# Key-value products of a linear-attention block: diagonal blocks of 32 by 32 instead of 64 by 64

## The chip, the cores and the metric

The kernel runs on one core of a Trainium2 chip. The metric is the device time of one execution in microseconds; the time before is the median of three runs, 482.34 us (482.19 to 482.75).

## The reference

One transformer block in float32 on a sequence of 2048 rows of 512 values, conditioned by a vector c (six modulation vectors sa, ca, ga, sb, cb, gb come from it).

```python
h = _layernorm(x) * (1 + ca) + sa
x = x + ga * A(h)                     # linear attention, 32 heads of 16 values
h = _layernorm(x) * (1 + cb) + sb
x = x + gb * B(h)                     # dense 512 -> 1792, mish, dense 1792 -> 512
# A:  q, k, v = h @ wqkv, by heads
phi = lambda t: where(t > 0, t + 1, exp(t)) + 1e-6
kv  = einsum("bhsd,bhse->bhde", phi(k), v)      # a 16 x 16 matrix for each head
z   = einsum("bhsd->bhd", phi(k))
num = einsum("bhqd,bhde->bhqe", phi(q), kv)
den = einsum("bhqd,bhd->bhq", phi(q), z) + 1e-6
A   = (num / den) @ wo
```

## The kernel before

The whole work is written out by hand: Python emits one instruction after the other, and each engine runs its own in that order, so the order in the program is the order of the work. Generators (`spawn`, `spawn_idle`, `tick`) put the work of the other engines between the matmuls of TensorE (PE): each `tick()` moves every running generator one `yield` on. DMAs are issued from SP's queue (hardware) and from GpSimd's (POOL, software). Large products are made of three float32r products of upper and lower halves (`mm3`, `split`: the upper half is a copy, mostly on ScalarE, ACT; the lower half a subtraction on VectorE, DVE). A few small products are done in plain float32; in the trace each of those calls leaves two weight-load records and two matmul records.

The sequence is worked on in blocks b of 512 rows and tiles t of 128. Up to some 103 us the kernel computes phi(k) and accumulates `gacc`, the 512 by 512 product of the normalized x and phi(k) over all rows. From it come `zs[k]` (four tiles of 128 by 512, `kv_side`, L1128), which stand for h transposed times phi(k). Then q is computed for blocks 0 and 1 (`q_sevens`, L1146; its last results are the `cq` of L408).

The place of the change is L1149 to L1166, at 125 to 132 us. In order of the program:
- `attend(0, 3)` begins (L1149): the denominators `den`, 16 float32 products with 32 weight columns and 128 moving columns, in four column blocks of the array (L926).
- `kv_ps` (L1151 to L1156): for each of four groups g of 128 columns (8 heads) and each k, the product of `wv[k]` and `zs[k]` for diagonal blocks only, 64 by 64 (j = 0, 1); 32 calls. The bank `kv_ps` is one of four of the tag `acc`.
- `run(early_rows[0])` (L1157): ACT and DVE finish splits of MLP weights (`a_0l`, `s_0l`).
- the masks (L1158 to L1162): VectorE multiplies the diagonal blocks by `bmask` (1 inside a head's 16 by 16 block, 0 outside) into `kv`, which was set to zero at the start (L154).
- `split` of kv: `kvh` on ScalarE, `kvl` on VectorE (L1163, L1166). Between the two, `attending` goes one step on: `rden` and its reciprocal on VectorE (L930, L931), `rden_d` to DRAM and `rd`, its broadcast, back (L933, L937), issued from GpSimd for blocks 0 and 1.

After it come q for block 2 (`q_unit`, three PSUM banks `h`), the products `m_ps` of kv and wo (L1179), `attend(1, 4)`, q for block 3, and then the output products `o_unit` (L974 to L983) whose weights are `qs`, the halves of phi(q) divided by its denominator (L945, L946, L88). The normalized rows of the first blocks are turned through VectorE's transposes (`wide_n`) and DMAs (`sq_n`); the small steps of that are `rs_n` (VectorE and GpSimd, L1001, L199), `nb_n` (L1004) and `n` (ACT, L208). `gb_row`, `gb_d`, `gb_bc` (L454 to L458) broadcast one modulation row over GpSimd's queue. At 192 us the MLP's first products `p_a` begin (`pairs_begin`, L1247), with `b_0l`, a lower half that VectorE makes (L88), and from there the MLP takes the rest.

Of the kernel before, what the change touches and what calls it, by code (L numbers as in the profile page):

```python
# [11 lines left out]
ALU = mybir.AluOpType  # L12

P = 128
# [11 lines left out]
def block_kernel(ctx: ExitStack, tc: tile.TileContext, x, wqkv, wo, w1, b1t, w2, c, wmodt, out):  # L26
    nc = tc.nc
    act, dve, pool, pe, sp = nc.scalar, nc.vector, nc.gpsimd, nc.tensor, nc.sync
# [13 lines left out]
    def ps(tag, name, shape=(P, 512)):  # L42
        return psp.tile(list(shape), F32, tag=tag, name=name, bufs=PBUFS[tag])
# [24 lines left out]
    def run(gen):  # L68
        for _ in gen:
            pass  # L70
# [7 lines left out]
    def split(name, t, keep, key, lo_engine=dve, hi_engine=act, plus=None):  # L78

        hi, lo = sb(f"{name}h", F32R, t.shape), sb(f"{name}l", F32R, t.shape)  # L80
        if hi_engine is act:
            act.activation(hi, t, AF.Copy)
        else:
            hi_engine.tensor_copy(hi, t)
        if lo_engine is dve:
            yield
        if plus is None:
            lo_engine.tensor_tensor(lo, t, f32(hi), op=ALU.subtract)  # L88
        else:
            dve.scalar_tensor_tensor(lo, t, plus, f32(hi), op0=ALU.add, op1=ALU.subtract)  # L90
        keep[key] = hi, lo
# [55 lines left out]
    bmask = cst.tile([P, P], F32, name="bmask")  # L147
# [540 lines left out]
    wv, wos = {}, {}  # L688
# [17 lines left out]
    zs = {}  # L706
# [444 lines left out]
    kv_ps = ps("acc", "kv_ps")  # L1151
    for g in range(4):
        for k in range(4):
            for j in range(2):
                cs = slice(P * g + 64 * j, P * g + 64 * (j + 1))
                pe.matmul(kv_ps[64 * j:64 * (j + 1), cs], wv[k][:, cs], zs[k][:, cs], start=k == 0, stop=k == 3)  # L1156
    run(early_rows[0])  # L1157
    for j in range(2):  # L1158
        js = slice(64 * j, 64 * (j + 1))
        dve.tensor_tensor(kv.rearrange("p (g m) -> p g m", g=4)[js, :, js],  # L1160
                          kv_ps.rearrange("p (g m) -> p g m", g=4)[js, :, js],
                          bmask[js, js].unsqueeze(1).to_broadcast([64, 4, 64]), op=ALU.mult)  # L1162
    kv_halves = split("kv", kv, kvs, 0)  # L1163
    next(kv_halves)
    next(attending)
# [500 lines left out]
```

## Time and profile before

| | |
|---|---|
| median of three runs | 482.34 us |
| the profiled execution | 482.34 us |
| its span, first to last instruction | 480.6 us |
| TensorE busy (matmuls) | 473.1 us, 98%, 2290 records |
| weight loads (PEld) | 387.9 us, 81%, 2290 records |
| VectorE busy | 392.1 us, 82% |
| ScalarE busy | 309.9 us, 64% |
| GpSimd busy | 135.9 us, 28% |

All views are of one profiled execution. PE is the matmul side of TensorE, PEld its weight loads, which run beside the matmuls; matmuls are pipelined, so records of one engine overlap. A timeline merges neighbouring records of one line and shape and gives their number (x64) and the time from the first start to the last end. "Idle before" is the time in which an engine stood still, with the instruction whose end released it; "issue" means that nothing in the profile explains it.

### The profile page before, as it was taken

The page shows a single profiled execution, that of the slowest core. Times are in us where ns is not written, and L with a number is a line of the kernel's source. Part 1 is how long each engine was busy: PE and PEld are TensorE (multiplying, and loading weights), DVE is VectorE, ACT ScalarE, POOL GpSimd, SP SyncE. Part 2 cuts the span into 40 slices and gives each one's busy share as a digit, 9 for nine tenths or more (in the row PEclk, how much of TensorE's full clock was granted, in tenths as well). Part 3 has the DMA queues.
Part 4 walks back from the last instruction along what each step waited for, and adds up shares of the span by engine and source line. Part 5 has one row for each costly group of instructions (what it writes and reads, how often), then busy time and mean ns, then how long its engine had stood idle before and what let it go on. Part 6 is the DMA issues. An engine that isn't in the chain of part 4 may idle for free.

```text
span 480.6 us, 7101 instructions
## 1 busy us (share of the span) xinstructions
PE 473.1 (98%) x2290; PEld 387.9 (81%) x2290; DVE 392.1 (82%) x786; ACT 309.9 (64%) x556; POOL 135.9 (28%) x233
## 2 busy tenths in 40 slices
PE   7999999999999999999999999999999999999997
PEld 6778786868887888888888888888888888888887
DVE  6989897998899899698879874798544787779992
ACT  6977558756667977587787756694156677637700
POOL 3586242000022255112224425343011101354400
PEclk9999999999999999999999999999999999999999
DMA  8904649443766356927538759999643503487974
GB/s 304 383 15 83 115 111 241 131 153 91 240 184 178 84 125 182 324 86 242 175 111 233 249 156 307 369 310 280 188 119 87 118 15 88 110 218 155 242 156 106
DMA packets 81280, 84.92 MB, mean 177 GB/s; under 512 B 23473, under 2 KB 55737, under 8 KB 81242
## 3 DMA queue, kind: packets, MB, share of 16 engines
q1 hardware_dynamic: 55176, 47.08, 34.0%
q0 software_dynamic: 23808, 36.59, 28.4%
q10 hardware_dynamic: 2258, 0.79, 0.8%
q8 instruction: 18, 0.29, 0.2%
q14 instruction: 20, 0.16, 0.1%
HBM read 55.32 MB, written 22.81 MB: 163 GB/s over the span
## 4 chain that ended last, share of the span: by engine, by line
PE 83%; DVE 5%; DMA 4%; POOL 2%; ACT 2%; issue 2%; SPq 1%; DVEq 0%; POOLq 0%; ACTq 0%
PE p_a L1234 15%; PE o L981 9%; PE p_s L1234 8%; PE oacc L74 5%; PE oacc L76 5%; PE oacc L75 5%; PE m L76 5%; PE m L74 5%; PE m L75 5%; PE p L1234 4%; PE pq_a L397 2%; DMA ku<-ku 2%; PE pq L74 2%; PE pq L76 2%; PE pq L75 2%
## 5 line engine op out<-in xcount | busy, mean ns | idle before, releaser
L1239 DVE TENSOR_TENSOR cb<-p_s,u 128x512 f32<-128x512 f32 x28 | 19.2, 687 | 12.2 <-ACT u L1287 10.6
L820 POOL DMA_DIRECT2D wb<-w2d x14 | 9.8, 704 | 65.2 <-PE m L76 28.3
L1226 ACT ACTIVATE ub<-cb,b1c 128x512 f32<-128x512 f32 x28 | 20.1, 720 | 9.0 <-DVE cb L1239 8.7
L1562 POOL DMA_DIRECT2D wt_m<-w2t x20 | 14.0, 702 | 25.1 <-PE m L76 16.8
L199 POOL TENSOR_TENSOR rs_n<-rs_n,half 128x1 f32<-128x1 f32 x16 | 9.7, 609 | 36.0 <-DVE rs_n L225 19.1
L1244 ACT ACTIVATE p<-p_a 128x512 f32<-128x512 f32 x12 | 7.0, 582 | 19.7 <-PE p_a L1234 11.7
L933 POOL DMA_DIRECT2D rden_d<-rden x2 | 1.5, 733 | 61.6 <-DVE rden L931 61.6
L1287 ACT ACTIVATE u<-p_a 128x512 f32<-128x512 f32 x14 | 8.4, 597 | 13.8 <-PE p_a L1234 13.6
L1201 ACT ACTIVATE u<-p,b1c 128x512 f32<-128x512 f32 x14 | 9.6, 684 | 11.7 <-PE p L1234 11.7
L1201 ACT ACTIVATE u<-p_a,b1c 128x512 f32<-128x512 f32 x14 | 9.6, 687 | 8.5 <-PE p_a L1234 8.3
L826 POOL DMA_DIRECT2D w2b<-w2d x20 | 10.6, 540 | 13.9 <-PE oacc L76 8.2
L270 ACT ACTIVATE hf_n<-sq_n,mc 128x512 f32<-128x512 f32 x16 | 12.0, 804 | 0.7 <-DMA w2r<-in_w_dram 0.7
L304 DVE SCALAR_TENSOR_TENSOR ku<-e_k,relu_k 128x512 f32<-128x512 f32 x16 | 10.9, 684 | 1.2 <-ACT relu_k L302 1.2
L304 DVE SCALAR_TENSOR_TENSOR q<-e_q,relu_q 128x512 f32<-128x512 f32 x16 | 10.7, 687 | 1.4 <-ACT relu_q L302 1.4
L199 POOL TENSOR_TENSOR rs_x<-rs_x,half 128x1 f32<-128x1 f32 (+1 forms) x10 | 7.8, 785 | 13.2 <-DVE rs_x L194 12.3
L190 DVE BATCH_NORM_STATS2 st_x<-x 128x6 f32<-128x512 f32 x13 | 8.8, 676 | 3.1 <-DMA x<-in_x_dram 3.1
L256 POOL DMA_DIRECT2D sq_n<-wide_n x16 | 8.7, 553 | 6.8 <-DVE wide_n L239 4.7
L175 DVE SCALAR_TENSOR_TENSOR wm<-wm,sc_row 128x512 f32<-128x512 f32 x16 | 10.5, 684 | 0.0
L945 DVE SCALAR_TENSOR_TENSOR q<-q,rd 128x512 f32<-128x512 f32 x16 | 10.4, 683 | 0.1
L256 POOL DMA_DIRECT2D sq_x<-wide_x x16 | 8.9, 566 | 5.0 <-DVE wide_x L239 4.6
L301 ACT ACTIVATE e_k<-pk 128x512 f32<-128x512 f32 x16 | 9.4, 590 | 1.3 <-PE pk L76 1.3
L759 DVE TENSOR_TENSOR w2g<-w2r,gb_bc 128x256 f32<-128x256 f32 x28 | 10.0, 416 | 0.0
(1622 smaller groups left out, 1884.8 us busy)
## 6 DMA issues: line engine op xcount, KB each, us to landing
wm<-in_wmodt_dram SPq DMA_DIRECT2D x24, 256.0 KB
w1p<-in_w_dram SPq DMA_DIRECT2D x24, 256.0 KB
w2b<-w2d POOLq DMA_DIRECT2D x20, 256.0 KB, 6.8
wt_m<-w2t POOLq DMA_DIRECT2D x20, 256.0 KB, 3.6
r<-in_x_dram SPq DMA_DIRECT2D x16, 256.0 KB
x<-in_x_dram SPq DMA_DIRECT2D x15, 256.0 KB
w2r<-in_w_dram SPq DMA_DIRECT2D x14, 256.0 KB
wb<-w2d POOLq DMA_DIRECT2D x14, 256.0 KB, 3.6
```

The source lines that it names most:

```text
L74: pe.matmul(o, st[0], mv[0], start=start, stop=False)
L75: pe.matmul(o, st[0], mv[1], start=False, stop=False)
L76: pe.matmul(o, st[1], mv[0], start=False, stop=stop)
L199: pool.tensor_tensor(y, y, half[:, lo:hi], op=ALU.pow)
L256: queues[n % len(queues)].dma_start(v[32 * m:32 * (m + 1), :, a, :], w[32 * a:32 * (a + 1), m:16:4].rearrange("p j t c -> p j (t c)"))
L304: dve.scalar_tensor_tensor(dst, e, 1.0, r, op0=ALU.min, op1=ALU.add)
L981: pe.matmul(p, l, r, start=not seeded and g == 0 and i == 0, stop=g == 3 and i == 2, skip_group_check=seeded)
L1201: act.activation(u, p, AF.Mish, bias=b1c[:, f:f + 1])
L1226: act.activation(u, p, AF.Mish, bias=b1c[:, f:f + 1])
L1234: pe.matmul(p, st, mv, start=onto is None and c == 0 and i == 0, stop=c == 1 and i == 2, skip_group_check=onto is not None)
L1239: dve.tensor_tensor(out, p, u, op=ALU.add)
L1562: pool.dma_start(v, w2t[g][:, :, SUM[name], :])
```

## The change

```diff
     for g in range(4):
         for k in range(4):
-            for j in range(2):
-                cs = slice(P * g + 64 * j, P * g + 64 * (j + 1))
-                pe.matmul(kv_ps[64 * j:64 * (j + 1), cs], wv[k][:, cs], zs[k][:, cs], start=k == 0, stop=k == 3)
+            for j in range(4):
+                cs = slice(P * g + 32 * j, P * g + 32 * (j + 1))
+                pe.matmul(kv_ps[32 * j:32 * (j + 1), cs], wv[k][:, cs], zs[k][:, cs], start=k == 0, stop=k == 3)
     run(early_rows[0])
-    for j in range(2):
-        js = slice(64 * j, 64 * (j + 1))
+    for j in range(4):
+        js = slice(32 * j, 32 * (j + 1))
         dve.tensor_tensor(kv.rearrange("p (g m) -> p g m", g=4)[js, :, js],
                           kv_ps.rearrange("p (g m) -> p g m", g=4)[js, :, js],
-                          bmask[js, js].unsqueeze(1).to_broadcast([64, 4, 64]), op=ALU.mult)
+                          bmask[js, js].unsqueeze(1).to_broadcast([32, 4, 32]), op=ALU.mult)
```

The products outside the heads' blocks are masked away in both versions, so fewer of them are computed: 64 calls with 32 weight columns and 32 moving columns in place of 32 calls with 64 and 64. A mask instruction covers 32 partitions and four groups of 32 columns, in place of 64 partitions and four groups of 64.

## Rows read from the trace of the kernel before

**Rows 1.** The page, busy us (share of the span) and records of TensorE.

```profile
PE 473.1 (98%) x2290; PEld 387.9 (81%) x2290; DVE 392.1 (82%) x786; ACT 309.9 (64%) x556; POOL 135.9 (28%) x233
```

**Rows 2.** Waits of weight loads, 126.4 to 478: us in total, times, longest.

```profile
PEld den L926 <- issue: 0.7, 2, 0.4
...
PEld den L926 <- DVE q L304: 0.4, 1, 0.4
...
PEld p_a L75 <- DVE b_0l L88: 0.2, 1, 0.2
PEld kv_ps L1156 <- issue: 0.2, 1, 0.2
```

**Rows 3.** By stretch: length, busy PE, PEld, DVE, ACT, POOL, clock, DMA share, GB/s.

```profile
126.40:153.70 27.30, 27.30 (x206) 22.49 (x203) 27.15 (x59) 16.64 (x35) 6.77 (x11) 1.00 0.64 186
...
192.40:477.30 284.90, 284.88 (x1296) 237.65 (x1295) 220.38 (x419) 172.04 (x303) 73.17 (x126) 1.00 0.68 187
```

**Rows 4.** TensorE, 125.3 to 128.5: timeline (start, length), then ns of one (min/median/max).

```profile
125.36 1.08 PE L926 MATMUL den<-q,hmask 128*32 128x128 f32 x32
126.37 2.08 PE L1156 MATMUL kv_ps<-zs,wv 128*64 128x64 f32 x64
...
L1156 PE MATMUL kv_ps<-zs,wv x64: 221/222/271, 126.4 to 128.2; 128*64 128x64 f32 x64
L926 PE MATMUL den<-q,hmask x128: 272/273/298, 125.4 to 172.9; 128*32 128x128 f32 x128
```

**Rows 5.** Timeline of den's weight loads up to 125.359, 125.385 and 125.410.

```profile
125.36 0.11 PEld L926 LDWEIGHTS den<-q,hmask 128*32 128x32 f32 x1 [0.35 <-issue]
...
125.36 0.13 PEld L926 LDWEIGHTS den<-q,hmask 128*32 128x32 f32 x4 [0.35 <-issue]
...
125.36 0.16 PEld L926 LDWEIGHTS den<-q,hmask 128*32 128x32 f32 x8 [0.35 <-issue]
```

**Rows 6.** Timeline of VectorE around the masks, 128.7 to 130.0.

```profile
128.76 0.42 DVE L88 TENSOR_TENSOR a_0l<-w1p,a_0h 128x256 fp32r<-128x256 f32 x1
...
129.10 0.85 DVE L1160 TENSOR_TENSOR kv<-kv_ps,bmask 64x256 f32<-64x256 f32 x2
...
129.98 0.35 DVE L930 TENSOR_SCALAR rden<-den,tiny_den 128x128 f32<-128x128 f32 x1
```

**Rows 7.** The masks alone: ns of one (min/median/max), first and last start.

```profile
L1160 DVE TENSOR_TENSOR kv<-kv_ps,bmask x2: 406/416/427, 129.1 to 129.5; 64x256 f32<-64x256 f32 x2
```

**Rows 8.** Timelines of VectorE and of TensorE's weight loads at 149.5 to 150.6.

```profile
149.48 0.69 DVE L88 TENSOR_TENSOR qs_2l<-q,qs_2h 128x512 fp32r<-128x512 f32 x1
...
150.55 0.19 PEld L981 LDWEIGHTS o<-m_2h,qs_2l 128*128 128x128 f32 x1
```

**Rows 9.** Timelines of GpSimd (143.9 to 157.7) and of VectorE at 158.3.

```profile
143.91 0.71 POOL L933 DMA_DIRECT2D rden_d<-rden  x1 [6.54 <-DVE rden L931]
...
157.10 0.59 POOL L458 DMA_DIRECT2D gb_bc<-gb_d  x1 [4.67 <-DMA gb_d<-gb_row]
157.70 0.60 POOL L199 TENSOR_TENSOR rs_n<-rs_n,half 128x1 f32<-128x1 f32 x1
...
158.33 0.16 DVE L1004 SCALAR_TENSOR_TENSOR nb_n<-osum,rs_n 128x1 f32<-128x1 f32 x1 [0.51 <-POOL rs_n L199]
```

**Rows 10.** Waits of ScalarE from 158 to 182: us, times, longest.

```profile
ACT n L208 <- DVE nb_n L1004: 3.8, 2, 2.9
```

**Rows 11.** Waits of VectorE from 126.4 to 195.

```profile
DVE wide_n L239 <- ACT n L208: 1.4, 2, 1.1
```

**Rows 12.** Timelines of VectorE and of TensorE's weight loads at 192 us.

```profile
191.67 0.69 DVE L88 TENSOR_TENSOR b_0l<-hf_n,b_0h 128x512 fp32r<-128x512 f32 x1
...
192.41 0.19 PEld L75 LDWEIGHTS p_a<-b_0l,a_0h 128*128 128x128 f32 x1 [0.21 <-DVE b_0l L88]
```

**Rows 13.** By stretch, as rows 3: the DMA share behind the masks.

```profile
136.50:147.50 11.00, 11.00 (x77) 8.75 (x76) 10.93 (x24) 5.81 (x11) 1.58 (x3) 1.00 0.99 285
```

**Rows 14.** Waits of SP's queue from 128 to 145: us, times, longest.

```profile
SPq L103 <- PE m_ps L76: 9.1, 2, 8.7
```

## The prediction

> **What bounds the kernel now.** I read the page's busy shares first: TensorE is busy 98% of the span [rows 1]. Shares say nothing of one stage, so the next view is what TensorE's weight loads waited for from 126.4 us, where the changed products begin, to the last matmul. Two entries name another engine. A den load waited 0.4 us for VectorE's q, but two other den loads show the same idle time as "issue", 0.7 us for both: that is TensorE's own change of array shape. A load for p_a waited 0.2 us for VectorE's b_0l, and this one I take as a wait [rows 2]. The table by stretch agrees: behind that wait TensorE is busy 284.88 of 284.90 us [rows 3]. So whatever moves TensorE's arrival there, or b_0l, moves the end by as much. The reader is to see two things at once: TensorE is the bound, and it meets VectorE at 192.4 us with nothing to spare. Before that, from 126.4 to 153.7, VectorE is itself busy 27.15 of 27.30 us [rows 3]: in the stage of the change there are two full engines.
>
> The profiled execution took 482.34 us around a span of 480.6, and 482.34 is also the median of the three runs, so the sum is made against it directly.
>
> **Part 1, the products.** 32 calls become 64, and as each call leaves two records (64 now), 64 records become 128. Now: the first record of kv_ps starts at 126.37 and they end 2.08 us later; one takes 0.222 us, so 31 steps of two (one for each column block) take 2.08 - 0.22 = 1.86 us, 0.060 us a step [rows 4]. The den products beside it have the array shape that the change will use, 32 columns, four blocks: 1.08 - 0.27 = 0.81 us over 7 steps of four is 0.116 us a step [rows 4]. At the granted clock of 1.00 [rows 3], the 2.4 GHz level, that is 278 cycles for 128 moving columns and 144 for 64, so about two cycles a column and some 0.007 to 0.009 us more. A step of four with 32 moving columns is then 64 cycles, 0.027 us, plus 0.008: 0.035 us. Another limit lies close: four den loads have started 0.02 us after the first, eight after 0.05 us, so some 0.007 us each [rows 5], and four of these are 0.028. Bounds for a step: 0.028 below, 0.116, den's whole step, above. I take 0.035, worked out from the two rows of the same engine and type. 31 steps: 1.09 us in place of 1.86, a gain of 0.77. Also, loads for kv_ps idle 0.20 us at the change from 32 columns to 64, where nothing but issue is named [rows 2]; with 32 columns behind 32 an ordinary step of 0.116 stands there, a gain of 0.09. The change of shape towards pq stays. **TensorE gains 0.86 us** (1.08 at the lower bound; at the upper it loses 1.65).
>
> **Part 2, the masks.** Two VectorE instructions of 64 partitions by 256 columns become four of 32 by 128. Now: 0.406 and 0.427 us [rows 7], together 0.85 us, and rden starts 0.88 after the first [rows 6]. They lie end to end. The 256-wide a_0l in front does not: it lasts 0.42 and kv starts 0.34 behind it [rows 6]. A column costs (0.68 - 0.42)/256 = 1.0 ns, by the 512-wide qs_2l [rows 8] and a_0l, so 128 columns less make 0.42 into 0.28. If end to end stays: four of 0.28 and four gaps of about 0.02 are 1.20 us, **0.32 more than 0.88**. If they overlap as a_0l and kv do: four steps of 0.34 - 0.13 = 0.21 are 0.84, 0.04 less. If rden's 0.35 for 128 columns from PSUM [rows 6] is the right length: 1.48, 0.60 more. I take +0.32: kv's own row is the nearest.
> The Trainium skill (VectorE: DVE Perf Modes, "Two Vector instructions with no wait between them") has a rule against this part: an instruction that starts on another group of 32 partitions than the one before it is held until all earlier ones have finished. By it three masks and rden are held instead of one mask and rden, and the sum would be the +0.32; without it, the -0.04.
>
> What is queued behind: on VectorE rden and all that follows, on ScalarE kvh, which reads kv, and on GpSimd the rden_d transfer. No DMA is added or moved, and the mask's constant is only sliced otherwise.
>
> **What each is worth at the end.** VectorE's queue from 126.4 to 153.7 has 0.15 us left for all its waits together [rows 3]: it gets next to nothing from TensorE's 0.86 us, and carries the 0.32 along. The first place where TensorE meets it: qs_2l runs 149.48 to 150.17 and its weight load starts at 150.55 [rows 8]. That is 0.38 us of room up to the load, and up to 0.19 more as far as the load, 0.19 long, runs ahead of the matmuls: I take the middle, 0.47, so TensorE can come 0.47 us earlier if VectorE stays, and 0.47 - 0.32 = 0.15 with the masks. The rest of the 0.86 turns into a wait for qs_2l.
> Then b_0l. I followed it back. VectorE's second rden releases GpSimd's rden_d at 143.91; behind its landing come the rd loads and gb_d, a wait of 4.67 us for gb_d's landing, gb_bc at 157.10 and rs_n at 157.70; for that VectorE idles 0.51 and goes on at 158.33 [rows 9]. From there the waits that I see are ScalarE's for VectorE's nb_n (3.8 us) [rows 10] and VectorE's for ScalarE's n (1.4 us) [rows 11]: the two release each other up to b_0l, 191.67 to 192.36, whose load starts at 192.41 [rows 12]. So +0.32 at rden is +0.32 at b_0l, if the transfer keeps its length. It may not: rden_d lands out of a full DMA system (0.99 busy from 136.5 to 147.5 [rows 13]), and part of this traffic is released on SP by TensorE's m_ps products [rows 14], which come 0.86 earlier. A transfer issued later into the same backlog lands less than 0.32 later. I keep +0.32 as the upper and 0 as the lower end, and as the issue itself moves by all of it, take 0.25.
>
> **Sum:** TensorE's 0.86 is lost at qs_2l and b_0l, and b_0l comes 0.25 later: 482.34 + 0.25 = 482.6 us.
>
> **The rivals.**
> - *TensorE's gain comes through* (faster side). It needs b_0l to come 0.86 earlier: 482.34 - 0.86 = 481.5, or 481.3 with 0.028 us a step. For it: TensorE is the bound at all other places. Against: VectorE's row without idle time [rows 3].
> - *The masks overlap.* Then VectorE is 0.04 earlier, and a DMA backlog that clears sooner may let 158.33 come up to 0.5 earlier (the idle 0.51 of [rows 9]). TensorE is still held by qs_2l, at 0.47 + 0.04 = 0.51 earlier: 482.34 - 0.04 = 482.3, or 481.8 at best.
> - *Issue becomes TensorE's bound* (slower side). kv_ps now passes one record per 0.030 us and den one per 0.029 (their steps over two and four); no row shows a lasting rate above that, only short bursts [rows 5]. If that is a limit per record, 128 records take 31 x 0.116 = 3.60 us, 1.65 more with the shape change, and as TensorE has nothing to spare at 192.4, the end is 1.65 later: 484.0. It decides from a step above 0.035 + 0.86/31 = 0.063 us on, where TensorE itself gets late. Against it: two cycles a column explains both rows by streaming alone.
> The Trainium skill (TensorE: Matmul & The Clock Gate, "Wait — 56ns, not 53.3ns?") states such a floor, about 25 ns from start to start however small a matmul is. By that rule 128 records would take 3.2 us and the end would be some 1.3 later. The 0.007 us between den's loads speaks against it as a floor over all four column blocks.
> - *A larger mask price*, 0.60, with the transfer in full: 482.9; inside my case.
>
> **How the numbers follow.** About 0.2%, 0.96 us, is what a measurement of this kernel can tell from no change. My case 0.72, overlapping masks 0.15, issue bound 0.07, TensorE's gain in full 0.06. My case runs from 482.3 (backlog hides it) to 482.9 and with the spread of the three runs of before (482.19 to 482.75) to 483.2; overlap reaches to 481.8. The range 481.8 to 483.2 leaves out the last two rivals. Slower by over 0.96 us: the issue bound and 0.02 of my case, 0.09. Faster by over 0.96 us needs the gain in full at the lower bound of a step, or the DMA timing to fall well: 0.04. The rest, 0.87, is no change.
>
> **What would show each step.** Right: 128 kv_ps records in about 1.1 us with no shape idle behind den; four masks end to end in about 1.2 us, kvh and rden 0.3 later; TensorE now waits for qs_2l (0.7 us, where it had none), and the p_a load still starts just behind b_0l, at 192.4 to 192.8. Wrong: TensorE without waits up to the end and a span of 479.7 (gain through); kv_ps over 3 us (issue); masks 0.2 apart (overlap); b_0l well ahead of its load (another wait decides).

## The result and the profile after

The changed kernel takes 484.03 us (median of 8 runs, 483.15 to 484.45), the kernel before 482.62 in the same comparison (8 runs). The ratio is 1.0029 with a 95% interval of 1.0021 to 1.0037: **slower by 1.4 us**, where 482.6 was forecast and 483.2 was the upper end (0.25 more than the 482.34 from which the forecast started). The profiled execution has a span of 482.5 us against 480.6, so the trace shows a loss of 1.9.

First the two edited parts. The timelines of TensorE and VectorE after, as [rows 4, 6]:

```profile
125.69 1.08 PE L926 MATMUL den<-q,hmask 128*32 128x128 f32 x32
126.59 1.28 PE L1156 MATMUL kv_ps<-zs,wv 128*32 128x32 f32 x128
127.80 0.50 PE L74 MATMUL pq<-hT_x_0h,wq_0h 128*128 128x512 f32 x1
...
129.10 0.42 DVE L88 TENSOR_TENSOR a_0l<-w1p,a_0h 128x256 fp32r<-128x256 f32 x1
129.43 1.18 DVE L1160 TENSOR_TENSOR kv<-kv_ps,bmask 32x128 f32<-32x128 f32 x4
130.65 0.35 DVE L930 TENSOR_SCALAR rden<-den,tiny_den 128x128 f32<-128x128 f32 x1
```

Note first that `den`, the last work ahead of the change, already starts 0.33 us later than in the profile of before (125.36): this one execution brought that along, and it has to be taken off every difference below. Then: 128 records of kv_ps in 1.28 us, and rden 1.22 us behind the first mask, where it was 0.88.

Next, what the weight loads waited for, from 120 to 480 us (in us in total, times, longest; [rows 2] has the same before, from 126.4):

```profile
PEld o L981 <- DVE qs_2l L88: 1.8, 2, 1.0
PEld den L926 <- issue: 1.1, 3, 0.4
PEld p_a L75 <- DVE b_0l L88: 0.8, 1, 0.8
```

TensorE now waits 1.8 us for qs_2l, in two waits (1.0 up to 150.9 us and 0.8 up to 192.5), and 0.8 in place of 0.2 for b_0l. Behind that it waits for nothing, as before. The chain to b_0l, in the timelines of GpSimd and VectorE and the last matmul of TensorE:

```profile
144.58 0.71 POOL L933 DMA_DIRECT2D rden_d<-rden  x1 [6.53 <-DVE rden L931]
150.91 2.36 POOL L937 DMA_DIRECT2D rd<-rden_d  x4 [5.62 <-ACT relu_q L302]
159.02 0.59 POOL L458 DMA_DIRECT2D gb_bc<-gb_d  x1 [5.22 <-DMA gb_d<-gb_row]
...
160.26 0.16 DVE L1004 SCALAR_TENSOR_TENSOR nb_n<-osum,rs_n 128x1 f32<-128x1 f32 x1 [0.66 <-POOL rs_n L199]
...
193.60 0.68 DVE L88 TENSOR_TENSOR b_0l<-hf_n,b_0h 128x512 fp32r<-128x512 f32 x1
...
478.92 0.28 PE L76 MATMUL m<-wt_m,l_m_4l 128*128 128x256 f32 x1
```

The same places before: GpSimd's first rd and the last matmul here, the rest in [rows 9, 12].

```profile
149.54 2.36 POOL L937 DMA_DIRECT2D rd<-rden_d  x4 [4.92 <-ACT gb_row L454]
...
477.00 0.28 PE L76 MATMUL m<-wt_m,l_m_4l 128*128 128x256 f32 x1
```

| step | later than before, us | added there |
|---|---|---|
| den (ahead of the change) | 0.33 | 0.33, this execution |
| rden_d issued (second rden) | 0.67 | 0.34, the masks |
| rd issued, behind rden_d's landing | 1.37 | 0.70, transfer |
| gb_bc issued, behind gb_d's landing | 1.92 | 0.55, transfer |
| nb_n, b_0l, last matmul | 1.93, 1.93, 1.92 | 0 |

So nothing more is lost behind 160 us, and TensorE lost nothing in its own work. Some 1.25 us come from two transfers that got longer, more than the masks cost.

A second path ends almost together with this one. VectorE's last product ahead of nb_n, q<-q,rd (L945), needs the rd loads; it ends at 157.82 before and at 159.59 after, 1.77 us later. Before and after, in VectorE's timeline:

```profile
153.73 1.50 DVE L945 SCALAR_TENSOR_TENSOR q<-q,rd 128x512 f32<-128x512 f32 x2
...
156.53 1.29 DVE L945 SCALAR_TENSOR_TENSOR q<-q,rd 128x512 f32<-128x512 f32 x2
```

```profile
154.66 0.69 DVE L945 SCALAR_TENSOR_TENSOR q<-q,rd 128x512 f32<-128x512 f32 x1 [0.19 <-DMA rd<-rden_d]
156.31 0.69 DVE L945 SCALAR_TENSOR_TENSOR q<-q,rd 128x512 f32<-128x512 f32 x1 [0.96 <-DMA rd<-rden_d]
...
158.31 1.28 DVE L945 SCALAR_TENSOR_TENSOR q<-q,rd 128x512 f32<-128x512 f32 x2
```

GpSimd's small rs_n ends 0.41 to 0.48 us behind the end of that q in all nine traces in which rs_n starts ahead of it and nb_n waits for rs_n, the one of before among them. So without gb_d's longer transfer nb_n would still have come some 1.7 us later (estimate: 1.77, less the 0.05 between the 0.48 of before and the 0.43 usual). Most of the loss is in rden_d (0.70) and in rd behind it (1.77 - 1.37 = 0.40); gb_d counts for some 0.2.

The view of DMA issues gives the same as time from issue to landing, for the kernel before and the changed one (stretch 142 to 160 us; KB each, median us):

```profile
rd<-rden_d POOLq DMA_DIRECT2D x4, 256.0 KB, 4.8
...
rden_d<-rden POOLq DMA_DIRECT2D x1, 64.0 KB, 5.1
gb_d<-gb_row POOLq DMA_DIRECT2D x1, 2.0 KB, 5.0
```

```profile
rd<-rden_d POOLq DMA_DIRECT2D x4, 256.0 KB, 5.2
...
rden_d<-rden POOLq DMA_DIRECT2D x1, 64.0 KB, 5.8
gb_d<-gb_row POOLq DMA_DIRECT2D x1, 2.0 KB, 5.5
```

Something else had moved the other way: SP's queue. Before and after, its loads in the full DMA stretch:

```profile
137.34 0.33 SPq L103 DMA_DIRECT2D wm<-in_wmodt_dram  x1
...
139.64 2.20 SPq L103 DMA_DIRECT2D wm<-in_wmodt_dram  x2
```

```profile
136.74 0.33 SPq L103 DMA_DIRECT2D wm<-in_wmodt_dram  x1
...
139.04 2.19 SPq L103 DMA_DIRECT2D wm<-in_wmodt_dram  x2
```

They wait for TensorE's m_ps [rows 14], so they come 0.60 us earlier, 0.93 without the 0.33. GpSimd's rden_d comes 0.67 later, behind them. That gave the theories. A: the early products release SP's loads, which stretch the chain's transfers, and the masks cost their own size (later D: what stretches the transfers is the load of SP's transfers). B: the masks' delay alone does it (later E: the late issue alone). C: it is chance.

One thing has to be added to A. The same eight SP loads (wm, r and w1p) are issued ahead of rden_d in both kernels, by 143.3 us. What differs is what they meet: before, the first of them is issued as GpSimd has just issued the rd loads of the block ahead (134.96 to 137.37 us); after, it comes 1.3 us before the end of these issues (135.64 to 138.05). The slowest of those rd loads took 9.4 us from issue to landing, 7.1 before.

### The profile page after: what moved, and what is told of

Read it like the earlier page. It is cut to its first block, busy times and chain, and to the rows that moved or that the text cites. A ratio compares the mean times of both kernels' runs of the same rounds, so it can differ in the third digit from the quotient of the medians.

```text
span 482.5 us, 7228 instructions
## 1 busy us (share of the span) xinstructions
PE 473.6 (98%) x2354; PEld 386.6 (80%) x2354; DVE 392.4 (81%) x788; ACT 310.0 (64%) x556; POOL 136.2 (28%) x233
## 4 chain that ended last, share of the span: by engine, by line
PE 72%; DVE 11%; DMA 5%; issue 4%; ACT 4%; POOL 3%; SPq 0%; DVEq 0%; POOLq 0%; ACTq 0%
PE p_a L1234 15%; PE p_s L1234 8%; PE oacc L76 5%; PE oacc L74 5%; PE oacc L75 5%; PE m L76 5%; PE m L74 5%; PE m L75 5%; PE p L1234 4%; PE pq_a L397 2%; DMA ku<-ku 2%; PE o L981 2%; PE pk L76 1%; DMA rden_d<-rden 1%; DMA gb_d<-gb_row 1%
## 5 line engine op out<-in xcount | busy, mean ns | idle before, releaser
L945 DVE SCALAR_TENSOR_TENSOR q<-q,rd 128x512 f32<-128x512 f32 x16 | 10.3, 682 | 1.1 <-DMA rd<-rden_d 1.1
```

## The experiments

Times are against the kernel before, run beside each on the same chip. The columns on the right are of one profiled execution each, whose own time stands beside the median: e12's and e7's are slow ones of their runs, e14's a quick one. "rden_d" is the second one's time from issue to landing, "b_0l to end" the distance from b_0l's start to the end of the last matmul.

| run | ratio (95%) | us, median | profiled, us | rden_d, us | b_0l starts | b_0l to end |
|---|---|---|---|---|---|---|
| before | | 482.62 | 482.34 | 5.1 | 191.67 | 285.61 |
| change | 1.0029 (1.0021 to 1.0037) | 484.03 | 484.26 | 5.8 | 193.60 | 285.60 |
| e1 masks only | 1.0017 (1.0008 to 1.0026) | 483.64 | 483.01 | 5.2 | 192.33 | 285.62 |
| e2 half the products | 1.0014 (1.0006 to 1.0023) | 483.39 | 483.32 | 5.8 | 192.63 | 285.62 |
| e7 change, two masks | 1.0016 (1.0006 to 1.0026) | 483.18 | 483.93 | 5.6 | 193.25 | 285.62 |
| e3 change, work put off | 0.9989 (0.9981 to 0.9998) | 482.11 | 482.63 | 3.3 | 191.95 | 285.62 |
| e4 before, work put off | 1.0005 (0.9996 to 1.0014) | 483.10 | 483.10 | 3.8 | 192.42 | 285.62 |
| e5 change, w1p late | 1.0126 (1.0112 to 1.0140) | 488.94 | 488.65 | 4.0 | 197.96 | 285.61 |
| e6 before, w1p late | 1.0109 (1.0095 to 1.0123) | 487.98 | 488.42 | 4.7 | 197.72 | 285.63 |
| e8 change, put off, w1p late | 1.0133 (1.0118 to 1.0149) | 489.01 | 488.34 | 3.0 | 197.63 | 285.65 |
| e9 change, w1p mid | 1.0017 (1.0008 to 1.0026) | 483.69 | 484.12 | 4.9 | 193.40 | 285.62 |
| e10 before, w1p mid | 0.9999 (0.9990 to 1.0008) | 482.45 | 482.16 | 4.0 | 191.33 | 285.77 |
| e11 change, put off, w1p mid | 1.0009 (0.9992 to 1.0026) | 482.63 | 482.60 | 3.0 | 191.89 | 285.65 |
| e12 change, on GpSimd | 0.9989 (0.9979 to 0.9998) | 482.39 | 483.16 | 6.1 | 192.45 | 285.62 |
| e13 before, on GpSimd | 0.9992 (0.9983 to 1.0000) | 482.50 | 482.50 | 4.7 | 191.70 | 285.74 |
| e14 change, r late | 1.0013 (1.0002 to 1.0024) | 483.19 | 482.36 | 3.6 | 191.63 | 285.63 |
| e15 before, r late | 0.9993 (0.9984 to 1.0002) | 482.17 | 482.09 | 3.8 | 191.37 | 285.66 |
| e16 change, r late, on GpSimd | 0.9987 (0.9977 to 0.9997) | 481.62 | 482.02 | 4.2 | 191.35 | 285.61 |
| e17 change, r late, put off | 1.0014 (1.0002 to 1.0027) | 483.25 | 482.64 | 3.2 | 191.96 | 285.63 |
| e18 before, r late, on GpSimd | 0.9992 (0.9983 to 1.0001) | 482.38 | 482.21 | 3.8 | 191.40 | 285.75 |

The last column is the first finding: where TensorE waits for b_0l, the end stands 285.60 to 285.65 us behind b_0l's start, whatever was done before it; where it does not wait (e8, e10, e13, e15, e18) the distance is 285.65 to 285.77. Where TensorE waits, b_0l sets the end.

**One half of the change at a time (e1, e2).** e1 leaves the products as before and has only the four masks. e2 has `range(2)` for k and `stop=k == 1` in the kernel before, so it leaves out half of the key-value sum; TensorE is early and VectorE is not late.

> The mask in four pieces of 32 rows, the products as before in blocks of 64. VectorE is late by the masks' 0.34 us, TensorE is not early, so SP's loads behind m_ps are issued as before. Theory A (TensorE's early products release SP's loads earlier, and these stretch the rden_d and rd transfers): the masks' delay alone costs its own size, +0.2 to +0.4 us, and rden_d and rd keep their lengths. Theory B (VectorE's late issue alone meets a worse moment of the DMA backlog): +1.2 to +1.6 us, all of the change's loss. Theory C (the longer transfers are what one run of DMA happened to do): 0 to +0.4.

> Only two of the four products of each group of key-value columns are made, in blocks of 64; two masks as before. It leaves out half of the key-value sum. TensorE is early by 16 steps of 0.060 us, 0.96 us, VectorE is not late. If the chain through rden keeps its times, TensorE waits for qs_2l and b_0l and the time is 0 to -0.3 us. Theory A: SP's loads come about 0.6 us earlier, rden_d and rd land later, +0.6 to +1.2 us. Theory B: 0 to -0.3. Theory C: 0 to -0.3.

Measured: +0.82 us by the ratio's 0.0017 for the masks, +0.68 for the early products, and 1.5 together, the change's 1.4. A had the second right and the first too small, B and C had both wrong. So each part of the change costs by itself; as each ratio is known to about 0.45 us, the shares are rough. The trace of e1: rden_d keeps its length (5.2) and is issued 0.43 us later (0.10 of it already ahead of the change), gb_bc comes 0.41 later, nb_n 0.66. The 0.24 between the last two seem to come from GpSimd's small rs_n, 0.60 us before [rows 9]:

```profile
157.51 0.59 POOL L458 DMA_DIRECT2D gb_bc<-gb_d  x1 [4.51 <-DMA gb_d<-gb_row]
158.12 0.84 POOL L199 TENSOR_TENSOR rs_n<-rs_n,half 128x1 f32<-128x1 f32 x1
```

But rs_n ends 0.43 us behind VectorE's last q (158.53), which stood still 0.39 us for rd: the delay came through rd and VectorE, not through gb_bc.

In e2 SP's loads come 0.65 us earlier (0.93 counted from den, which starts 0.28 later there) and rden_d takes 5.8 us, as in the changed kernel, though VectorE's work is that of before:

```profile
136.69 0.33 SPq L103 DMA_DIRECT2D wm<-in_wmodt_dram  x1
```
```profile
rden_d<-rden POOLq DMA_DIRECT2D x1, 64.0 KB, 5.8
```

**TensorE early without the masks' price (e7).** The first product of each group covers 64 moving columns, so that two masks of 64 rows do as before. Against the changed kernel, the masks' lines left out:

```diff
-    pe.matmul(kv_ps[32 * j:32 * (j + 1), cs], wv[k][:, cs], zs[k][:, cs], start=k == 0, stop=k == 3)
+    ms_ = cs if k else slice(P * g + 64 * (j // 2), P * g + 64 * (j // 2 + 1))
+    pe.matmul(kv_ps[32 * j:32 * (j + 1), ms_], wv[k][:, cs], zs[k][:, ms_], start=k == 0, stop=k == 3, ...)
```

> The changed kernel, but the first product of each group writes 64 columns for each 32 rows, so that the two masks of 64 rows can be used as before: TensorE gains 0.66 in place of 0.86 us (8 steps at 0.060 in place of 0.035), VectorE gains and loses nothing. If the two halves of the change add up, this is the run with half of the products again, a little weaker: +0.3 to +0.6 us. If the loss needs the masks, 0 to -0.2.

Measured +0.77 (0.0016), somewhat above the range, rden_d 5.6 us: early products cost by themselves, with all of them made.

**VectorE's stretch relieved (e3, e4).** In the changed kernel and in the one before:

```diff
-    run(early_rows[0])
...
+    spawn_idle(early_rows[0])
     act.preload_act_table_set("mish")
```

> The changed kernel with what is left of columns_early's first part (VectorE and ScalarE work of about 2 us) taken out of the full VectorE stretch ahead of the masks and queued as idle work for later. rden and its transfer start 1 to 2 us earlier than in the changed kernel. All theories that put the loss on the chain rden, rden_d, rd, gb_d, b_0l expect TensorE's gain to come through: 0.5 to 0.9 us below the kernel before, so 1.9 to 2.3 below the changed one. If the loss sat elsewhere (TensorE itself), it would stay at +1 to +1.4.

> The kernel before with the same work taken out of the stretch. TensorE waited only 0.2 us for b_0l there: 0 to -0.3 us against the kernel before. The difference between this kernel and the changed one with the same edit is then TensorE's own gain, 0.5 to 0.9 us. If the early release of SP's loads costs by itself whatever VectorE does, the two are alike within 0.3 us.

e3 is 0.5 us *below* the kernel before by its ratio (0.7 by medians), 1.9 below the changed kernel: the loss is gone, so it did not sit in TensorE's own work. It is not a test of VectorE alone: in the trace of e3 SP's last wm loads come at 133.3 to 137.3 us, in place of 139.0 to 141.2, and the DMA engines are 0.45 busy from 142 to 150 us, in place of 0.95. e4 came out at +0.24, inside its interval of no change and above what was expected. The trace of e4 says why: nb_n comes 1.2 us earlier than before, but the subtractions that were put off stand on VectorE at 170 us, and b_0l starts at 192.42, 0.75 later. In e3 they stand there too, so e3 still waits 0.8 us for b_0l.

**The w1p loads later (e5, e6, e8, e9, e10, e11).** `spawn_idle(early_rows[1])` moves from its place at g == 1 to behind tile t == 2 (e5, e6, e8, "w1p late") or to t == 1 (e9, e10, e11, "w1p mid") of the o_unit loop; e8 and e11 have e3's edit as well.

> The changed kernel, with early_rows[1] queued four units later: its two w1p loads (256 KB each, 141.9 and 142.5 us in the changed kernel) leave the full DMA stretch that the second rden_d has to come through, and so does some VectorE work behind them from 160 to 170 us. Nothing else is changed, VectorE's masks and TensorE's early products stay. Theory D (what lengthened the rden_d and rd transfers is the load of SP's transfers ahead of them in the DMA engines): the second rden_d, which landed at 150.4 us, lands 0.8 to 1.5 us earlier (512 KB at the 390 GB/s of that stretch is 1.3 us), and the time falls by 0.7 to 1.8 us against the changed kernel, to between -0.4 and +0.7 us against the kernel before. Theory E (the transfers are longer because GpSimd issues them later, whatever else moves): rden_d lands within 0.3 us of where it did, and the time stays at +1.1 to +1.6.

> The kernel before with the same two loads later. rden_d lands earlier by 0.8 to 1.5 us by theory D, but TensorE waited for b_0l only 0.2 us there: -0.3 to +0.2 us against the kernel before, so the time is bounded by TensorE. Theory E: no change.

> The changed kernel with columns_early's rest out of the full VectorE stretch (as in e3) and the w1p loads late (as in e5). Theory D: both help the same chain; TensorE can gain at most its 0.86 us plus the 0.2 us it waited for b_0l, so 0.7 to 1.1 us below the kernel before, unless VectorE's work that was put off meets b_0l from 165 to 192 us, which would leave it where e3 was, -0.5 to -0.8. Theory E: as e3, -0.5 to -0.8.

The transfer did what D said in e5, where it landed at 148.5 in place of 150.4 us, and hardly moved in e6 (148.9, 149.0 before). The time did not: ratios 1.0126, 1.0109 and 1.0133, 5 to 6 us slower. The loads came to stand behind the third rden_d in SP's queue, were issued at 165.4, and VectorE's queue stood behind their landing, in e5:

```profile
172.97 0.43 DVE L846 TENSOR_TENSOR s<-w1p 128x256 f32<-128x256 f32 x1 [5.85 <-DMA w1p<-in_w_dram]
```

> The changed kernel, with early_rows[1] queued two units later, so that its w1p loads stay ahead of the third rden_d in SP's queue (in e5 they came behind it, and VectorE's queue stood behind their landing). They are issued once their buffers come free, some microseconds after 142 us. Theory D (SP's transfers in the DMA engines lengthen rden_d and rd): the second rden_d lands 0.8 to 1.9 us earlier than the 150.4 us of the changed kernel, GpSimd's gb_bc as much earlier, and the time is 0.5 to 1.5 us below the changed kernel, between -0.1 and +0.9 us against the kernel before. If the w1p loads land late again, VectorE waits for them at s and the time is above the changed kernel. Theory E (the lateness of the issue alone): +1.1 to +1.6.

> The same in the kernel before. TensorE waited for b_0l only 0.2 us there: by theory D -0.3 to +0.2, by E the same.

> The changed kernel with both: columns_early's rest out of the full VectorE stretch (as in e3) and the w1p loads two units later (as in e9). If VectorE's work that was put off does not meet b_0l, TensorE's gain comes through in full: 0.8 to 1.1 us below the kernel before; if it does, as e3, 0.5 to 0.8 below.

e9: 1.0017 (1.0008 to 1.0026), half a microsecond better than the change by the ratio, at the upper end of D's range. rden_d took 4.9 in place of 5.8 us, but the second rden came 0.94 later than in the changed kernel (0.29 of it there from the beginning of this execution), as VectorE waited for the first block's rd at 142 us. e10: 0.9999, as expected. e11: 1.0009 (0.9992 to 1.0026), so no gain; nb_n came 4.0 us earlier than in the changed kernel and b_0l only 1.7, because VectorE's later stretch holds what was put off.

**VectorE relieved without putting work off (e12, e13).** The four subtractions ahead of the masks go to GpSimd (an engine argument for `split` in `rows`, for its first call alone). SP's loads keep their place.

> The changed kernel, with the four subtractions that stand ahead of the masks on VectorE (the low parts a_0l and s_0l, 2.1 us from 127.3 to 129.4 us) on GpSimd, which does nothing from 76 to 132 us. Nothing is put off into a later VectorE stretch, as it was in e3. If b_0l sets the end and VectorE's stretch from 127 us sets b_0l through rden, rden_d and rd, then b_0l comes 2 us or more earlier than in the changed kernel, TensorE no longer waits for it, and TensorE's gain comes through: 0.8 to 1.2 us below the kernel before, with the last matmul no longer 285.6 us behind the start of b_0l. If GpSimd's work holds up rden_d or slows VectorE down, the time is at or above the kernel before.

> The same in the kernel before. TensorE waited for b_0l 0.2 us and for nothing else there: 0 to -0.4 us. The difference between this and e12 is what the changed products are worth to TensorE where no other engine meets it: 0.8 us by the step of 0.035 in place of 0.060 us. If the early release of SP's transfers costs by a way of its own (not through b_0l), the two differ by less than 0.4.

e12 is 0.5 us below the kernel before, short of the 0.8 to 1.2; e13 0.4 below. So the two are alike, and the gain is that of the edit: with VectorE relieved, the change costs nothing that these runs can tell. In e12's trace TensorE still waits 0.8 us for b_0l, which comes 1.15 earlier than in the changed kernel, not 2. In that trace rden_d is issued 0.47 us *earlier* than in e13 and lands later. Of e12, then e13, GpSimd's issue and the DMA view:

```profile
143.09 0.71 POOL L933 DMA_DIRECT2D rden_d<-rden  x1 [6.01 <-DVE rden L931]
...
rden_d<-rden POOLq DMA_DIRECT2D x1, 64.0 KB, 6.1
```
```profile
143.56 0.71 POOL L933 DMA_DIRECT2D rden_d<-rden  x1 [6.88 <-DVE rden L931]
...
rden_d<-rden POOLq DMA_DIRECT2D x1, 64.0 KB, 4.7
```

The two differ by the change alone; SP's first load in the stretch is at 136.62 in e12 and at 137.58 in e13. A later issue is no explanation of the longer transfer here, nor in e5, where rden_d landed 1.9 us earlier than in the changed kernel; that speaks against E. The two are one execution each, and e12's is a slow one (483.16 against a median of 482.39).

**Loads taken out of the stretch (e14 to e18).** The row loads of the last block move behind the stretch, and no engine's work changes its order:

```diff
-        load_x(3, g, "r")
...
             if b == 1:
+                load_x(3, t, "r")
                 spawn(norm_first(1, t))
```

> The changed kernel, with the last four row loads (r of the last 512 rows, 256 KB each, of which two are issued at 137.2 and 138.1 us and are first read after 175 us) taken out of the full DMA stretch and issued some 30 us later. VectorE's and TensorE's work stays in its order. Theory D (SP's transfers ahead of rden_d and rd in the DMA engines set how late these land, and through them b_0l and the end): the second rden_d lands 1 us or more earlier than in the changed kernel, b_0l starts earlier by as much or until VectorE's own work decides, and the time falls by 0.8 to 2 us, to between +0.5 and -0.8 us against the kernel before. Theory E (not the load but something else in the change makes them late): +1.1 to +1.6. If a late r load holds up the sq_n transfers behind it in SP's queue, the time is above the changed kernel and the waits say so.

> The same in the kernel before: TensorE waited 0.2 us for b_0l there, so 0 to -0.3 us by theory D, and 0 by E.

In e14 rden_d takes 3.6 us, 2.2 less than in the changed kernel, with the changed products and masks in place. b_0l starts at 191.63, where it was before the change, and the span is 480.6. Its waits, from 110 to 480 us:

```profile
PEld o L981 <- DVE qs_2l L88: 1.0, 1, 1.0
...
PEld p_a L75 <- DVE b_0l L88: 0.3, 1, 0.3
```

So **the load of SP's transfers sets the length of rden_d**: that part of D is shown. The time does not follow. The ratio gives +0.63 us (0.1 to 1.2), just above D's range; the 12 runs lie from 482.09 to 485.14, wider than the changed kernel's own, and the trace is of one near the lower end (482.36). What the longer ones wait for was not seen. e15 gave 0.9993, 0.3 us below the kernel before, at the end of its range. So against e15, which has the same edit, the change still costs 1.0 us.

> The changed kernel with the r loads late and the four subtractions on GpSimd (e12). Theory D: both act on the same chain, so b_0l no longer holds TensorE and its 0.86 us come through: 0.7 to 1.1 us below the kernel before. Theory E: as e12, -0.3 to -0.7.

> The changed kernel with the r loads late and columns_early's rest put off (e3). VectorE is full again from 165 to 192 us with what was put off, so b_0l may hold TensorE as in e3: -0.5 to -1.1 us against the kernel before.

> The kernel before with both edits of e16, so that the two differ by the change alone. If TensorE bounds this one and b_0l no longer holds e16 by more than it did, the change is worth up to TensorE's 0.86 us: this is 0 to -0.5 us against the kernel before, and e16 is 0.4 to 0.9 us faster than this. If e16 owes its gain to the edits alone, this one is as fast: -0.7 to -1.1.

e16, r late and the subtractions on GpSimd, is the fastest median, 481.62 against 482.55, ratio 0.9987 (0.9977 to 0.9997): **it beats both kernels**, as e3 and e12 do, though by intervals that end close to 1. By the ratio the 0.6 us are what E expected; the median's 0.9 would be D's. TensorE waits only 0.3 us for qs_2l but still 0.8 for b_0l, so not all of its gain is through. The same edits without the change (e18) give 0.9992 (0.9983 to 1.0001). The 0.2 to 0.6 us between them, by ratios or medians, would be what the change is worth there; the intervals overlap, and it stays open. e17 missed its range: 1.0014 (1.0002 to 1.0027), with runs from 481.79 to 484.89, and no cause was found.

**Every edit beside its own control.** What the change costs with the same edit on both sides, by the ratios:

| edit on both sides | change, against before | without the change | difference, us |
|---|---|---|---|
| none | 1.0029 | | +1.4 |
| w1p late (e5, e6) | 1.0126 | 1.0109 | +0.8 |
| w1p mid (e9, e10) | 1.0017 | 0.9999 | +0.9 |
| r late (e14, e15) | 1.0013 | 0.9993 | +1.0 |
| subtractions on GpSimd (e12, e13) | 0.9989 | 0.9992 | -0.1 |
| both (e16, e18) | 0.9987 | 0.9992 | -0.2 |
| work put off (e3, e4) | 0.9989 | 1.0005 | -0.8 |

By the spread of the runs a difference is good to about 0.6 us, that of e5 and e6, of four runs each, to 0.9. Taking SP's loads away leaves 0.8 to 1.0 us of the loss, though it shortens rden_d; relieving VectorE ahead of the masks removes it, with SP's loads in place (e12). So a short rden_d in the trace did not bring the time back, and what the loss needs, by these runs, is VectorE's full stretch. How the lengthened transfers and that stretch work together was not settled.

## Why the prediction was wrong, point by point

- **Part 1, the products: right.** (1.28 - 0.196)/31 = 0.035 us a step, the value taken; the idle time at the change of shape is gone. pq's first record comes at 127.80, 0.59 earlier than before, 0.92 without the 0.33: 0.86 was forecast. The issue-bound rival is excluded: a record per 0.0088 us, over 128. The floor of some 25 ns that it drew from the Trainium skill (TensorE: Matmul & The Clock Gate, "Wait — 56ns, not 53.3ns?") does not hold here for records that alternate over four column blocks; the measurement decides.
- **Part 2, the masks: right.** Four of 0.27 to 0.30 us, end to end, rden 0.34 later; +0.32 was forecast. The overlap rival is excluded. The rule of the Trainium skill on held instructions (VectorE: DVE Perf Modes, "Two Vector instructions with no wait between them") agrees with 1.22 us from first mask to rden.
- **Where it arrives: right.** TensorE's gain turned into waits for qs_2l (0.97 at the first, 0.7 forecast) and b_0l, and the chain rden, rden_d, rd, nb_n, b_0l was followed correctly; from nb_n on every step is 1.93 later. The last column of the table confirms the end of it. What it missed is that rd reaches nb_n by two ways, through gb_d and gb_bc and through VectorE's q, and in most traces the second ends last.
- **The step that failed** is this: "A transfer issued later into the same backlog lands less than 0.32 later. I keep +0.32 as the upper and 0 as the lower end, and [...] take 0.25." The backlog was taken as given, though the sentence ahead says that part of it is released by TensorE; that part came 0.93 us earlier. The transfer got longer, not shorter. The term measured +0.34 for the masks, passed on in full (e1: rden_d 5.2 us against 5.1), plus 0.70 for rden_d and 0.55 for rd and gb_d behind it in the profiled run. In medians that is 1.4 in place of 0.25, with a part from each half of the change (e1 0.8, e2 0.7). Why an earlier release lengthens a transfer that had the same loads ahead of it before stays open.
- **The range** left out a transfer that grows. Its upper end was the masks' bound of 0.60 and the scatter of the runs. No rival had the price of TensorE's own gain as a loss: the one on the slower side looked at issue, and came to 484.0 by the wrong mechanism; that it stands so close to the 484.03 is luck.
- **The chances** of slower, 0.09, were too low for the same reason.

That SP's loads lengthen rden_d is shown by taking loads away (e14, e15, and e5 and e10 for the w1p loads). That TensorE's lead lengthens the transfers is borne out by the pairs: rden_d takes 5.6 to 6.1 us with the early products (change, e2, e7, e12) and 4.7 to 5.2 without (before, e1, e13), where all loads are in place (with w1p late e5 and e6 go the other way, 4.0 and 4.7); and the slowest rd load of the block ahead takes 7.7 to 9.4 us with them and 5.5 to 7.5 without, in all 15 traces in which no work is put off. That the 0.93 us of SP's lead is the way is argued; a run that holds SP's loads back and changes nothing else was not made. And that the longer transfers are the whole of the lost time is not shown: e14 has them short and still costs 1.0 us more than e15.

## What to carry to other kernels

Before costing a gain on an engine that waits later, list what its earlier progress releases: here buffers that SP's queue was waiting for, and with them loads that go into the DMA engines beside the chain that decides. A gain that is lost at a wait is not always worth zero: here it cost 0.7 to 0.8 us (e2, e7). And the masks' delay ahead of a full DMA system was passed on whole (e1): give such a delay no discount unless a row shows one.

When one engine's stretch is full, moving work off it beats saving time on another: e3, e12 and e16 gained with the same change that lost by itself, and e13 gained 0.4 us without the change. Set such a run beside its own control before crediting the change. And look where the moved work lands: in e4, e5 and e11 VectorE's later queue ate the gain.

## What the runs showed of the hardware that was not expected

- GpSimd's rden_d, 64 KB, took 3.0 (e8, e11) to 6.1 us (e12) from issue to landing with the same bytes. The Trainium skill (DMA: Bandwidth & Descriptors, "Issuing engines are not separate DMA queues") says that transfers from all issuing engines run on the same 16 DMA engines and interleave; these runs agree, 5.8 us with SP's r loads in the stretch (change) and 3.6 without them (e14).
- GpSimd's rs_n on 128 by 1 elements, in the same place of the program, took 0.60 us in the changed kernel and in the one before, 0.84 in e1 and 1.16 in e13. By the traces it is held by VectorE's q<-q,rd beside it: in the nine traces counted above it ends 0.41 to 0.48 us behind that q, however early it started; where it starts behind q's end, it takes 0.59 (e7) and 0.60 us (change). No run varied this alone.
- A 512-wide subtraction takes 0.69 us on VectorE and 1.30 to 1.73 on GpSimd (e12); a 256-wide one 0.42 and 0.74.
